# First batch of a random-feature attention and softplus block: the query features are turned before the division, and one product yields numerator and denominator

## The chip, the cores and the metric

One Trainium2 chip, one core. The metric is device time in microseconds (us) of the whole kernel, as the median of several executions. One execution is also profiled. In the profile PE is TensorE's matmul, PEld its weight load, DVE is VectorE, ACT is ScalarE, POOL is GpSimd and SP is the queue that issues transfers.

## The reference

```python
def phi(x):                                   # q and k, 8 batches x 8 heads x 576 tokens x 64
    proj = einsum('bhsd,md->bhsm', x, omega)  # 128 features
    h = proj - sum(x*x, -1)/2
    return exp(h - max(h, -1)) / sqrt(m)
q_p, k_p = phi(q_s), phi(k_s)
kv = einsum('bhsm,bhsd->bhmd', k_p, v)
z  = sum(k_p, axis=2)
num = einsum('bhsm,bhmd->bhsd', q_p, kv)
den = einsum('bhsm,bhm->bhs', q_p, z)[..., None] + 1e-06
x = transpose(num / den)                      # 4608 tokens x 512
h = x @ w_in                                  # 512 x 2048
out = (max(h, 0) + log1p(exp(-abs(h)))) @ w_out
```

All is float32. The two large products are made of three products each of rounded parts (a high and a low part of each operand).

## The kernel before

A "quad" is four heads of one batch, so there are 16 quads, two for each batch; the first batch is quads 0 and 1. A quad's 576 tokens are cut into five units `u` of 128 tokens (the last has 64 tokens, packed two heads deep, so it has half the instructions). The planner `in_order` takes a list of pieces of work (`do(engine, cost, due, emit, ...)`), each with an estimated cost, a due time, the pieces that it must follow (`after`) and the buffers that it takes and gives back, and writes one fixed order for all engines: at each step it picks an engine by the earliest start, and on that engine the startable piece with the earliest due time. A piece with two engines goes to the one that would end it first. `with_fill` puts idle matmuls (`fill`) into gaps of TensorE that it foresees, up to 228 us. The constants at the top (`AHEAD`, `LATE`, `PATIENCE`, `KEYS`, `QUERIES`, `IN`, `OUT`, `SPREAD`, `GAP`, `PACE`, and the offsets in `due + ...`) are these due times and margins.

In the first batch `plan_unit` loads a unit, projects it (`project`, lines 416 and 425), finds maxima and takes exponentials (line 454). Keys go on to `plan_early_keys`: `outer` (line 685) sums `kv` with its column of ones, `z` (line 700) and `high` (line 704) take it out of PSUM, `rows` (line 710) spreads z over all partitions by four matmuls, and `copy` (line 717) writes it as `zb`. Queries go to `plan_queries`: `den` (line 753) makes one multiply-and-sum of features and `zb` for each head on VectorE, `invert` (line 758) and `divide` (line 762) scale the features, `turn` (line 769) transposes them on TensorE, `turned` (line 781) copies them out, and `plan_x` multiplies them with `kvs` (line 871) for 256 or 320 tokens at once, which gives x with channels on the partitions, split into `xh` (line 883) and `xl` (line 887).

Later batches turn their features through memory instead, and stay on that way. The matmuls of the two large layers are lines 926 to 928 (`h`) and 955 to 957 (`acc`); the first two blocks of 256 tokens run side by side. The 32 weight pieces arrive in a packed form, and `plan_weights` unpacks and splits each on ACT, DVE and POOL (lines 306, 314, 317, 323, 326).

Of the kernel before, what the change touches and what calls it, by code (L numbers as in the profile page):

```python
# [10 lines left out]
F32 = mybir.dt.float32  # L11
# [34 lines left out]
PATIENCE = {"PE": 0.01, "DVE": 0.00, "ACT": 0.01, "POOL": 2.67, "SP": 0.97}  # L46
# [3 lines left out]
IN = (-36.40, -29.38, -35.24, 13.38, 39.26, -0.84, 18.43, 58.59, 71.95, 37.26, 72.53, 83.69, 168.77, 73.35, 60.09, 181.84)  # L50
OUT = (12.11, -3.45, -3.16, 37.83, 15.70, 36.06, 71.88, 74.85, 65.23, 26.71, 122.09, 40.54, 79.80, 155.65, 126.67, 119.25)
SPREAD = ((0, 24.76), (15.62, 68.69))
# [141 lines left out]
def favor_softplus_kernel(ctx, tc, q0, k0, qx, qy, kx, ky, vv, om, wi, wo, out):  # L194
# [37 lines left out]

    omf = const.tile([P, M], F32, name="omf")
# [54 lines left out]
    def plan_weights(nm, fc, due):  # L288
# [36 lines left out]
        def low_part(e):  # L325
# [5 lines left out]
            "SP", dma(0.65, 1.27, 1.7), due + 28.00, load, spare={} if last else {"w": 2},  # L331
# [5 lines left out]
        a = do(("ACT", "DVE"), (aw, dw2), due + 0.07, low_bits, after=[l], port=True)  # L337
        b = do("ACT", aw, due - 3.08, rebias, after=[l])
        c = do("DVE", dw, due + 2.51, joined, after=[a, b], port=True)
        d = do(  # L340
            ("ACT", "DVE"), (aw, dw2), due - 14.00, high_part, after=[c] + (in_w if last else []), take=[("w", box, "w")], port=True,
# [3 lines left out]
        return do(("DVE", "POOL"), (dw, pw), due - 10.48, low_part, after=[d], give=[(box, "raw")], port=True)  # L345


    class Quad:
        def __init__(self, n):
            self.b, self.qd = divmod(n, NQ)  # L350
            self.n, self.nm = n, f"_{self.b}_{self.qd}"
            self.kvm = self.zc = self.kvl = self.features = None
            self.keys, self.key_deps, self.part, self.sums = [], [], None, 0
            self.qt = ({}, {})
            self.turned, self.nums, self.slots = [], [], {}
            self.last = None
# [3 lines left out]
    def plan_unit(q, kind, us, due, early):  # L360
# [84 lines left out]
        def exponent(j):  # L445
# [12 lines left out]
            "SP", read(size), due + 9.90, load, behind=prev.get("load"),  # L458
# [3 lines left out]
        if kind == "k" and not early:  # L462
            for i in range(len(us)):
                ldv.append(do(
                    "SP", dma(0.7, 1.0, 0.7), due - 13.94, lambda i=i: load_v(i), behind=ld, take=[("v", b, ("vs", i))]
                ))
        s = do(("POOL", "ACT"), (pool(w), act(w)), due + 21.13, squares, after=[ld])
        r, sm = None, [("sm", b, "sms")]
        if not cols:
            r = do("DVE", dve(w), due + 115.69, norms, after=[s], behind=prev.get("norms"), take=sm)  # L470
# [3 lines left out]
            "PE", 0.19 + (0.46 if cols else 0.23) * nt, due - 6.73, project, after=[ld] + ([s] if cols else []),  # L474
# [5 lines left out]
        for j in range(2):  # L480
            e = do("DVE", dve(nt * M), due + 6.43, lambda j=j: maxima(j), after=[p] + ([r] if r and not j else []), behind=None if not j else e, give=[(b, "x")] if j and not early else [])
            es.append(e)
        e = do("DVE", 0.13, due - 29.30, less_norms, after=es, port=True)
        e = do("DVE", 0.13, due - 11.07, bias, after=[e], port=True)
# [9 lines left out]
        if kind == "k":  # L494
            plan_keys(q, us, due, b, es, ldv, early)
            return
        for i in range(len(us)):
            plan_queries(q, us[i], due - 7.44 * i, b, es, f"{nm}_{i}", i, i == len(us) - 1)

    def plan_split(q, kind, u, due):  # L500
# [59 lines left out]
        def exponent(t):  # L560
# [4 lines left out]
            "SP", read(n * (P + D) * P * 4), due - 77.07, load, behind=prev.get("load"), take=[("x", b, "x")],  # L565
        )
        prev["load"], ldv = ld, []
        if kind == "k":
            ldv = [do("SP", dma(0.7, 1.0, 0.7), due + 3.89, load_v, behind=ld, take=[("v", b, ("vs", 0))])]
        s = do(("POOL", "ACT"), (pool(n * D), act(n * D)), due + 7.71, squares, after=[ld])  # L570
        h = do(("ACT", "DVE"), (act(n * P), dve(n * P, 2)), due + 1.60, rounded, after=[ld], take=[("ts", b, "ts")], port=True)
        h = do(("DVE", "POOL"), (dve(n * P) + 0.12, 1.12 * pool(n * P)), due - 17.24, rest, after=[h, parted], give=[], port=True)
        r = do(
            "DVE", dve(n * D), due + 32.73, norms, after=[s, h], behind=prev.get("norms"), take=[("sm", b, "sms")],
# [10 lines left out]
        for t in range(n // 2):  # L585
            a = do(
                "ACT", act(2 * M, PSUM), due + 4.07, lambda t=t: aside(t), after=[p], behind=a,
                take=[] if t else [("ph", b, ("phs", 0))], spare={"ph": 1}, soon={} if t or n < 4 else {p: 0.22},
            )
            es.append(do("DVE", dve(2 * M), due - 13.77, lambda t=t: join(t), after=[a], give=[(b, ("ppb", t))]))  # L590
        m = do("DVE", dve(n * M), due + 26.68, maxima, after=es + [r])
        m = do("DVE", 0.33, due - 19.46, bias, after=[m], port=True)
# [20 lines left out]
    def plan_sums(q, keys, due, deps):  # L613
# [46 lines left out]
        for k, (b, i, u) in enumerate(keys):  # L660
            m = do(
                "PE", (0.86 if u < 4 else 0.43) + (0.0 if k else 0.09), due - 53.57, lambda k=k: outer(k), after=[m] if k else [x for x, _ in deps],
# [520 lines left out]
```

## Time and profile before

| | before |
|---|---|
| time, median of 3 | 1020.04 us (1019.51 to 1021.16) |
| profiled execution, time | 1019.18 us |
| profiled execution, span | 1017.4 us |
| mean granted TensorE clock | 0.994 of full |
| PE busy | 1005.5 us (99%) |
| PEld busy | 836.5 us (82%) |
| DVE busy | 764.1 us (75%) |
| ACT busy | 743.9 us (73%) |
| POOL busy | 106.2 us (10%) |

The span runs from the first to the last instruction; the time is 1.8 us longer. Busy shares are averages over the whole span: the first 80 us and the rest look different, and the rows below show both. In a line of the timeline the columns are start, length, engine, line and operation, and in brackets the idle time before it; the length of a matmul reaches past the start of the next, so that the pace is read from start to start. One float32 matmul that is no transpose stands as two records.

### The profile page before, as it was taken

The numbers are of one execution on the slowest core, as the hardware profiler recorded it, in microseconds if no ns is written. First come the engines' busy times: TensorE is split into PE (matmuls) and PEld (weight loads), VectorE is DVE, ScalarE is ACT, GpSimd is POOL, SyncE is SP. The second block draws the span as 40 slices with busy tenths as digits, with TensorE's granted clock in tenths as the row PEclk, the third lists the DMA queues.
The fourth block names the chain that finished last, engine by engine and source line by source line (L and its number), as shares of the span: only waits on it lengthen the run. The fifth ranks groups of instructions, "written<-read, shape, count | busy, mean of one in ns | idle before, by whom it ended". The sixth has DMA issues, their size and how long they took to land.

```text
span 1017.4 us, 17261 instructions
## 1 busy us (share of the span) xinstructions
PE 1005.5 (99%) x5424; PEld 836.5 (82%) x5424; DVE 764.1 (75%) x2320; ACT 743.9 (73%) x1857; POOL 106.2 (10%) x125
## 2 busy tenths in 40 slices
PE   8989999999999999999999999999999999999998
PEld 6768888888888888888788888888888878888886
DVE  5999977788979887889888878979798783223222
ACT  7999977777868776877778777877787765444443
POOL 1032113011001011001000110101001120000000
PEclk7999999999999999999999999999999999999999
DMA  9944245435354444445454354535263332001001
GB/s 339 374 151 151 71 144 144 135 105 144 109 169 132 123 133 148 130 112 137 120 157 122 112 141 128 164 105 159 73 189 106 96 101 83 1 1 42 1 1 41
DMA packets 117610, 124.48 MB, mean 122 GB/s; under 512 B 16272, under 2 KB 93712, under 8 KB 117520
## 3 DMA queue, kind: packets, MB, share of 16 engines
q1 hardware_dynamic: 117520, 123.39, 41.2%
q8 instruction: 43, 0.70, 0.3%
q14 instruction: 47, 0.39, 0.1%
HBM read 97.37 MB, written 25.98 MB: 121 GB/s over the span
## 4 chain that ended last, share of the span: by engine, by line
PE 95%; ACT 2%; DVE 1%; DMA 1%; SPq 0%; issue 0%; DVEq 0%
PE acc L955 13%; PE h L926 13%; PE acc L956 13%; PE acc L957 13%; PE h L927 13%; PE h L928 13%; PE kv_True L626 4%; PE xp L876 3%; PE ppq L538 3%; PE ppk L538 3%; PE kv_False L626 2%; PE ppq L416 1%; PE kv L685 1%; PE ppk L416 1%; DMA xq<-q 1%; DMA xk<-k 0%
## 5 line engine op out<-in xcount | busy, mean ns | idle before, releaser
L926 PE MATMUL h<-xh,wi 128*128 128x512 f32 (+1 forms) x640 | 238.4, 372 | 0.9 <-ACT qq L781 0.6
L927 PE MATMUL h<-xl,wi 128*128 128x512 f32 (+1 forms) x640 | 236.0, 369 | 0.0
L928 PE MATMUL h<-xh,wi 128*128 128x512 f32 (+1 forms) x640 | 235.8, 368 | 0.0
L955 PE MATMUL acc<-wo,gh 128*128 128x512 f32 x576 | 230.1, 400 | 0.0
L956 PE MATMUL acc<-wo,gh 128*128 128x512 f32 x576 | 225.5, 391 | 0.0
L957 PE MATMUL acc<-wo,gl 128*128 128x512 f32 x576 | 224.9, 390 | 0.0
L941 DVE SCALAR_TENSOR_TENSOR u<-h,u 128x512 f32<-128x512 f32 (+1 forms) x160 | 101.0, 632 | 113.0 <-ACT u L938 111.8
L932 ACT ACTIVATE u<-h 128x512 f32<-128x512 f32 (+1 forms) x160 | 89.2, 558 | 114.9 <-PE h L928 114.0
L945 ACT CAST gh<-u 128x512 fp32r<-128x512 f32 (+1 forms) x157 | 90.8, 579 | 65.7 <-DVE u L941 22.0
L926 PEld LDWEIGHTS h<-xh,wi 128*128 128x128 f32 x640 | 120.6, 188 | 22.1 <-DVE u L941 0.8
L928 PEld LDWEIGHTS h<-xh,wi 128*128 128x128 f32 x640 | 120.5, 188 | 20.6
L927 PEld LDWEIGHTS h<-xl,wi 128*128 128x128 f32 x640 | 120.7, 189 | 18.4
L955 PEld LDWEIGHTS acc<-wo,gh 128*128 128x128 f32 x576 | 108.3, 188 | 26.3 <-issue 7.1
L957 PEld LDWEIGHTS acc<-wo,gl 128*128 128x128 f32 x576 | 108.2, 188 | 24.0 <-DVE gl L949 0.4
L949 DVE TENSOR_TENSOR gl<-u,gh 128x512 fp32r<-128x512 f32 (+1 forms) x148 | 98.4, 665 | 37.6 <-ACT gh L945 33.2
L956 PEld LDWEIGHTS acc<-wo,gh 128*128 128x128 f32 x576 | 108.5, 188 | 18.0
L938 ACT ACTIVATE u<-u 128x512 f32<-128x512 f32 (+1 forms) x160 | 95.3, 596 | 2.3
L935 ACT ACTIVATE u<-u 128x512 f32<-128x512 f32 (+1 forms) x160 | 95.0, 594 | 2.7
L762 POOL TENSOR_TENSOR phq<-phq,dnq 128x512 f32<-128x512 f32 (+1 forms) x50 | 49.9, 1000 | 396.4 <-DVE dnq L758 290.7
L562 ACT ACTIVATE phk<-phk,smk 128x128 f32<-128x128 f32 x216 | 70.4, 392 | 12.1 <-DVE smk L558 11.8
L753 DVE CUSTOM_DVE_ANT_0 restq<-phq,zb 128x128 f32<-128x128 f32 x280 | 70.9, 290 | 8.4 <-ACT phq L562 4.8
L562 ACT ACTIVATE phq<-phq,smq 128x128 f32<-128x128 f32 x216 | 70.0, 392 | 4.0 <-DVE smq L558 3.9
(127 smaller groups left out, 1418.8 us busy)
## 6 DMA issues: line engine op xcount, KB each, us to landing
xk<-ky SPq DMA_DIRECT2D x48, 384.0 KB
xq<-qy SPq DMA_DIRECT2D x48, 384.0 KB
qdq<-restq SPq DMA_DIRECT2D x56, 256.0 KB
out<-o SPq DMA_DIRECT2D x36, 256.0 KB
vk<-vv SPq DMA_DIRECT2D x70, 130.0 KB
rawi<-wi SPq DMA_DIRECT2D x16, 512.0 KB
rawo<-wo SPq DMA_DIRECT2D x16, 512.0 KB
q<-qdq SPq DMA_DIRECT2D x64, 128.0 KB
```

What stands on the lines that cost most here:

```text
L562: nc.scalar.activation(b["ph"][:, c], b["ph"][:, c], AF.Exp, bias=b["sm"][:, 2, c : c + 1])
L926: nc.tensor.matmul(b["h"], wh, xh[:, cc, t], start=cc == 0, stop=False)
L927: nc.tensor.matmul(b["h"], wh, xl[:, cc, t], start=False, stop=False)
L928: nc.tensor.matmul(b["h"], wl, xh[:, cc, t], start=False, stop=cc == NCC - 1)
L935: nc.scalar.activation(b["u"], b["u"], AF.Exp, scale=-1.0)
L938: nc.scalar.activation(b["u"], b["u"], AF.Ln, bias=1.0)
L941: nc.vector.scalar_tensor_tensor(b["u"], b["h"], 0.0, b["u"], ALU.max, ALU.add)
L945: (nc.scalar.copy if e == "ACT" else nc.vector.tensor_copy)(b["gh"], b["u"])
L949: (nc.vector if e == "DVE" else nc.gpsimd).tensor_tensor(b["gl"], b["u"], b["gh"].bitcast(F32), ALU.subtract)
L955: nc.tensor.matmul(acc[tt], gh, w2[fc][:, 0], start=fc == 0, stop=False)
L956: nc.tensor.matmul(acc[tt], gh, w2[fc][:, 1], start=False, stop=False)
L957: nc.tensor.matmul(acc[tt], gl, w2[fc][:, 0], start=False, stop=fc == NFC - 1)
```

## The change

In the first batch the query features are no longer divided. `plan_early_queries` turns them on TensorE as they are, copies them out, and multiplies each head's turned features (now the stationary operand) with `kvs`, which holds the 64 columns of kv and z as a 65th: `num` gives numerator and denominator with tokens on the partitions. `invert` and `divide` then divide on VectorE, half as many elements as before. `plan_early_x` turns the quotient on TensorE (transposes of 128x128; for the last unit two matmuls with `stack`, two identities on top of each other) and splits it into `xh` and `xl`. So x of the first batch comes in three pieces of 256, 256 and 64 tokens for each quad, not in two of 256 and 320. `rows` and `copy` (the spread z) are gone. The last weight pieces' loads no longer wait for the product of quad 1. Nearly all due times and margins have other values.

```diff
-AHEAD = 375.50
+AHEAD = 374.44
-LATE = {"num": 1.22, "turn": 67.09, "project": 1.24, "blocks": 0.00, "out": 0.62, "in": 4.17, "store": 0.76, "outer": 0.20}
+LATE = {"num": 1.22, "turn": 66.91, "project": 1.24, "blocks": 0.00, "out": 0.81, "in": 4.17, "store": 1.97, "outer": 0.00}
-KEYS = ((-37.35, -23.60, -64.29, -37.35, -19.23), (-24.09, -26.58, -11.38, -11.52, -26.04))
-QUERIES = ((-156.79, -22.43, 15.03, 26.83, 24.93), (-27.14, -25.41, -47.26, 24.27, 28.98))
+KEYS = ((-34.89, -10.13, -62.32, -19.84, -30.15), (-27.37, -13.75, -11.38, -11.52, -45.48))
+QUERIES = ((-147.95, -33.19, 13.91, 26.44, 25.73), (-28.86, -31.76, -44.16, 21.32, 31.30))
-    GAP = 19.32
-    PACE = 4.69
+    GAP = 17.56
+    PACE = 4.80
...
+    stack = const.tile([P, D], F32, name="stack")
+    nc.vector.tensor_tensor(stack, eye[:, :D], eye[:, D:], ALU.add)
...
         def z():
-            q.z = z_wide[int(q.slots["z"][-1])][:, :4]
-            nc.vector.tensor_scalar(q.z, q.kv[:, :, 2 * D - 1], rm, None, ALU.mult)
+            x = at.tile([P, 4 * M], F32, name=f"kvs{q.nm}", tag=q.slots["zb"], bufs=1)
+            q.kvs = x[:, : 4 * (D + 1)].rearrange("p (c d) -> p c d", d=D + 1)
+            nc.vector.tensor_scalar(q.kvs[:, :, D], q.kv[:, :, 2 * D - 1], rm, None, ALU.mult)
-        def rows():
-            q.zp = bank(f"zp{q.nm}", q.slots["zp"])
-            for c in range(4):
-                nc.tensor.matmul(
-                    q.zp[:, c * M : (c + 1) * M], q.z[:, c : c + 1].broadcast_to([P, P]), ident,
-                    start=True, stop=True,
-                )
-        def copy():
-            q.zb = at.tile([P, 4, M], F32, name=f"zb{q.nm}", tag=q.slots["zb"], bufs=1)
-            nc.scalar.copy(q.zb.rearrange("p c m -> p (c m)"), q.zp)
...
+    def plan_early_queries(q, u, due, b, es, nm):
+        n = 4 if u < 4 else 2
+        def turn():
+            b["tp"] = bank(f"tp{nm}", b["tpb"]).rearrange("p (c m) -> p c m", m=M)
+            for c in range(n):
+                nc.tensor.transpose(b["tp"][:, c], b["ph"][:, c], ident)
+        def turned(e):
+            (nc.scalar.copy if e == "ACT" else nc.vector.tensor_copy)(b["junk"][:, :n], b["tp"][:, :n])
+        def num():
+            b["y"] = wide(bank(f"xn{nm}", b["yb"]))
+            for c in range(n):
+                o, h = (slice(c, c + 1), slice(c, c + 1)) if u < 4 else (slice(2 * c, 2 * c + 2), slice(c, 4, 2))
+                nc.tensor.matmul(b["y"][:, o], b["junk"][:, c], q.kvs[:, h], start=True, stop=True)
+        def invert():
+            dn = b["dn"] = at.tile([P, 4, 4], F32, name=f"dn{nm}", tag=b["dns"], bufs=1)
+            nc.vector.tensor_scalar(dn[:, 0], b["y"][:, :, D], 1e-6, None, ALU.add)
+            nc.vector.reciprocal(dn[:, 1], dn[:, 0])
...
+        def divide():
...
+            nc.vector.tensor_tensor(x, y, d, ALU.mult)
+        t = do("PE", 0.092 * n + 0.02, due + 9.98, turn, after=es, heat=256 * n, behind=prev.get("turn"), take=[("any", b, "tpb")])
+        h = do(("ACT", "DVE"), (act(n * M, PSUM), dve(n * M)), due - 43.63, turned, after=[t], give=[(b, "tpb")])
+        m = do(
+            "PE", 0.23 * n, due - 12.99, num, after=[h, q.kvl], heat=512 * n, take=[("any", b, "yb")],
+            behind=q.nums[-1] if q.nums else None, give=[(q.slots, "zb")] if u == NU - 1 else [],
+        )
+        i = do("DVE", 0.32 + (0.16 if u == 4 else 0), due - 58.05, invert, after=[m], take=[("dn", b, "dns")])
+        d = do("DVE", 0.09 + dve(4 * D), due - 54.18, divide, after=[i], give=[(b, "yb"), (b, "dns")])
...
+    def plan_early_x(q, due, o, rows, tail, nm):
+        w = D if tail else 2 * P
+        def turn():
+            y["x"] = bank(f"xp{nm}", y["b"])[:, : 2 * w].rearrange("p (a t) -> p a t", t=w)
+            for i, (b, _) in enumerate(rows):
+                for a in range(2):
+                    if tail:
+                        nc.tensor.matmul(y["x"][:, a], b["x_"][:, a], stack, start=True, stop=True)
+                    else:
+                        nc.tensor.transpose(y["x"][:, a, i * P : (i + 1) * P], b["x_"][:, a], ident)
+        def high(e):
+            (nc.scalar.copy if e == "ACT" else nc.vector.tensor_copy)(part(xh), y["x"])
+        def low():
+            nc.vector.tensor_tensor(part(xl), y["x"], part(xh).bitcast(F32), ALU.subtract)
...
-        if q.n == 1:
-            last_raw[1 if o else 0].behind = a
```

## Rows read from the trace of the kernel before

**Rows 1.** Windows: stretch, its length, busy us by engine (instructions), granted clock, DMA.

```profile
40.00:50.00 10.00, 9.64 (x73) 7.08 (x71) 9.27 (x48) 9.64 (x30) 2.14 (x2) 1.00 0.89 345
50.00:60.00 10.00, 8.21 (x63) 6.45 (x62) 9.68 (x43) 10.00 (x25) 3.77 (x3) 1.00 0.55 159
60.00:70.00 10.00, 8.65 (x63) 6.42 (x63) 9.90 (x42) 9.52 (x30) 3.40 (x4) 1.00 0.53 191
70.00:80.00 10.00, 9.43 (x78) 8.38 (x77) 9.87 (x23) 9.76 (x31) 0.92 (x1) 1.00 0.44 159
...
80.00:200.00 120.00, 120.00 (x827) 103.89 (x827) 98.16 (x303) 101.19 (x284) 23.68 (x26) 1.00 0.43 124
```

**Rows 2.** Windows of the fill matmuls alone (PE, PEld).

```profile
40.00:50.00 10.00, 1.40 (x4) 0.60 (x4) 1.00 0.89 345
50.00:60.00 10.00, 0.72 (x2) 0.30 (x2) 1.00 0.55 159
```

**Rows 3.** Windows of 2 us where the granted clock falls and comes back.

```profile
12.00:14.00 2.00, 0.04 (x1) 0.04 (x1) 1.94 (x6) 2.00 (x7) 0.00 (x0) 0.51 1.10 357
...
22.00:24.00 2.00, 2.00 (x19) 2.00 (x18) 1.93 (x4) 2.00 (x6) 0.00 (x0) 0.93 1.04 405
```

**Rows 4.** Timeline of PE, 0 to 90 us.

```profile
13.96 1.73 PE L416 MATMUL ppk<-omf,xk 64*128 64x128 f32 x8 [2.33 <-DMA xq<-q]
...
18.69 2.91 PE L1076 MATMUL fill<-ident 128*128 128x512 f32 x6
...
39.35 1.12 PE L685 MATMUL kv<-xk 128*128 128x128 f32 x8
40.30 0.60 PE L769 MATMUL tpq<-ident,xq 128*128 128x128 f32 x4
40.74 1.04 PE L685 MATMUL kv<-xk 128*128 128x256 f32 x4
...
43.85 1.08 PE L871 MATMUL xp<-qq,kvs 128*64 128x256 f32 x8
44.86 1.16 PE L710 MATMUL zp<-ident,z 128*128 128x128 f32 x8
45.77 0.70 PE L1076 MATMUL fill<-ident 128*128 128x512 f32 x2
...
51.41 0.63 PE L769 MATMUL tpq<-ident,xq 128*128 128x128 f32 x4 [1.41 <-DVE xq L762]
...
57.05 0.36 PE L926 MATMUL h<-xh,wi 128*128 128x256 f32 x1
...
75.22 0.39 PE L926 MATMUL h<-xh,wi 128*128 128x256 f32 x1 [0.57 <-ACT qq L781]
...
78.18 2.79 PE L626 MATMUL kv_True<-vk,phk 128*128 128x65 f32 x24
80.80 1.56 PE L626 MATMUL kv_False<-vk,phk 128*128 128x65 f32 x12
82.29 1.30 PE L871 MATMUL xp<-qq,kvs 128*64 128x320 f32 x8
```

**Rows 5.** Timeline of DVE: first of 16 sums in a run, and what follows.

```profile
46.96 0.29 DVE L753 CUSTOM_DVE_ANT_0 xq<-xq,zb 128x128 f32<-128x128 f32 x1
...
50.37 0.30 DVE L758 RECIPROCAL dnq<-dnq 128x4 f32<-128x4 f32 x3
...
55.92 0.75 DVE L887 TENSOR_TENSOR xl<-xp,xh 128x256 fp32r<-128x256 f32 x2
```

**Rows 6.** Groups by line, 0 to 80 us: count, busy us, mean ns, idle before.

```profile
L753 DVE CUSTOM_DVE_ANT_0 xq<-xq,zb 128x128 f32<-128x128 f32 (+1 forms) x40 | 10.5, 314 | 0.3 <-ACT xq L454 0.2
...
L762 POOL TENSOR_TENSOR xq<-xq,dnq 128x512 f32<-128x512 f32 (+1 forms) x5 | 5.3, 1077 | 31.9 <-DVE dnq L758 31.9
...
L762 DVE TENSOR_TENSOR xq<-xq,dnq 128x512 f32<-128x512 f32 x5 | 4.5, 893 | 0.0
```

**Rows 7.** The tile zb: count, duration ns min/median/max, first and last start.

```profile
L717 ACT COPY zb<-zp x2: 586/620/655, 36.2 to 46.3; 128x512 f32<-128x512 f32 x2
```

More of the change, by code (lines that the diff above doesn't have):

```diff
@@ L344, in plan_weights @@
             in_w.append(d)
[L345 removed]
+        return do(("DVE", "POOL"), (dw, pw), due - 13.42, low_part, after=[d], give=[(box, "raw")], port=True)
     class Quad:
@@ L457, in plan_unit @@
         ld = do(
-            "SP", read(size), due + 9.90, load, behind=prev.get("load"),
+            "SP", read(size), due + 9.68, load, behind=prev.get("load"),
             take=[("w" if early else "x", b, "x")], spare={"w": 2} if early else {},
@@ L564, in plan_split @@
         ld = do(
-            "SP", read(n * (P + D) * P * 4), due - 77.07, load, behind=prev.get("load"), take=[("x", b, "x")],
+            "SP", read(n * (P + D) * P * 4), due - 79.58, load, behind=prev.get("load"), take=[("x", b, "x")],
         )
@@ new lines, in plan_queries @@
+        d = do("DVE", 0.09, due + 4.11, invert, after=[d])
+        v = do(("POOL", "DVE"), (1.0 * f, dve(n * M)), due - 7.14, divide, after=[d], give=[(b, "dns")], port=True)
+        t = do("DVE", dve(n * M) + 0.03, due - 58.50, blocks, after=[v], port=True, late=LATE["blocks"], give=[(bu, ("phs", first))])
+        q.turned.append(
+            do("SP", dma(0.3, 0.95, 1.2, 1 if u < 4 else 2), due + 76.27, out_blocks, after=[t], give=[(bu, ("rest", first))], late=LATE["out"])
+        )
+        for o, w in chunks(q.b):
+            if (o + w - 1) // P != u:
+                continue
+            qc = {}
+            sizes = [w] if w <= 320 else [256, w - 256]
+            kinds = ["q" if w <= 256 else "q1"] if w <= 320 else ["q0", "q1"]
+            t = do(
+                "SP", dma(0.0, 0.0124 * w, 1.4, 4 * len(sizes)), due - 0.33, lambda qc=qc, o=o, sizes=sizes: in_blocks(qc, o, sizes),
+                after=list(q.turned), take=[(k, qc, ("tag", i)) for i, k in enumerate(kinds)], late=LATE["in"],
+            )
+            turned, q.turned = q.turned, [t]
+            plan_x(q, due, o, w, any_, qc, len(kinds))
+            q.turned = turned
@@ L841, in plan_queries @@
         t = do(
-            "PE", 0.092 * n, due + 5.12, turn, after=[v], heat=256 * n, behind=prev.get("turn"), give=[(bu, "x")] if last else [],
-            take=[(any_, b, "tpb")] + ([("q1" if u else "q0", qt, "tag")] if u in (0, 2) else []),
-            late=LATE["turn"] if q.b > 1 else 0,
-        )
-        prev["turn"] = t
-        h = do(
-            ("ACT", "DVE"), (act(n * M, PSUM), dve(n * M)), due - 46.49, turned, after=[t], give=[(b, "tpb")],
-        )
-        q.turned.append(h)
@@ L851, in plan_queries @@
-        if u not in (1, 4):
-            return
-        ch = 0 if u == 1 else 1
-        o, w = (0, 256) if ch == 0 else (256, 320)
-        plan_x(q, due, o, w, any_, qt)
-        q.turned = []
+            "PE", 0.23 if tail else 0.46, due - 36.01, turn, after=[d for _, d in rows], heat=1024, behind=prev.get("turn_x"),
+            take=[("any", y, "b")], give=[(b, "x") for b, _ in rows],
+        )
+        prev["turn_x"] = t
+        h = do(("DVE", "ACT"), (dve(2 * w), act(2 * w, PSUM)), due - 86.10, high, after=[t])
@@ L858, in plan_x @@
+        l = do("DVE", dve(2 * w), due - 89.86, low, after=[h], give=[(y, "b")])
+        for p in range(2):
+            x_lows[o, 2 * q.qd + p] = w, l
     def plan_x(q, due, o, w, any_, qt, nq=1):
```

182 lines of the change are left out of this document (79 added, 103 removed).

## The prediction

> **What bounds the kernel now.** I read the windows first, because busy shares over the whole span mix two stages. From 80 to 200 us PE is busy for all 120.00 us at full clock [rows 1]: there it is the limit, and work taken off another engine is worth nothing. Before that it is not. From 40 to 80 us PE is busy for 9.64, 8.21, 8.65 and 9.43 us of each 10, so it idles for 4.07 us, while DVE is busy for 38.7 of the 40 us and ACT for 38.9 [rows 1]. Of PE's busy time there, 1.40 and 0.72 us are fill matmuls, which compute nothing [rows 2]. So PE has 4.07 + 2.12 = 6.2 us without useful work between 40 and 80 us, set by DVE and ACT. The PE timeline names the places: it waits 1.41 us at 51.41 for a divide on DVE, and 0.57 us at 75.22, its last wait, for a copy on ACT [rows 4]. The first step of the large layer that has both quads' x stands at 57.05 [rows 4]. There is another soft stretch at the start: PE waits 2.33 us before 13.96 and runs 2.7 us of fill from 18.69 [rows 4], and the granted clock falls to 0.51 in 12 to 14 us and is back, at 0.93, in 22 to 24 us [rows 3]: half clock (1.2 GHz of 2.4) for about ten microseconds after an idle PE.
>
> So the account is PE's. After about 75 us it never waits, and the end moves by useful PE work added, less the empty PE time that disappears before.
>
> **The change part by part. PE, removed.** Four products with the divided features: one of 256 tokens takes 1.01 us from start to start (43.85 to 44.86); one of 320 tokens is 1.30 us long, less the same 0.07 us of overlap 1.23 [rows 4]. Two of each: 4.5 us. The spread of z takes 0.91 us (44.86 to 45.77) [rows 4], twice: 1.8 us. Together 6.3 us. The 36 transposes of features stay.
>
> **PE, added.** The product with numerator and denominator has 16 full and 2 x 2 half-unit matmuls a quad: 32 and 4 in all, each two records with 65 columns (130 in the last units) and 128 columns of weights. That shape is in the trace: 24 records of kv_True take 78.18 to 80.80, 0.109 us each; eight records of kv, entry included, take 0.95 us (39.35 to 40.30), 0.119 us each [rows 4]. I take 0.115: eight units of eight records at 0.92 us, 7.4 us. The two last units have four records of 130 columns: between 0.44 us (at 0.109) and the 1.04 us that four records of 256 columns last [rows 4]; by their closeness to 65 I take 0.5, 1.0 us together. So 8.4 us, with ends of 7.85 and 9.7. Turning the quotient: four transposes take 0.44 us (40.30 to 40.74) [rows 4], four times, and two last pieces of four records at 0.115: 1.8 + 0.9 = 2.7 us. Net 8.4 + 2.7 - 6.3 = **+4.8 us**, with ends of +4.2 and +6.1.
>
> The Trainium skill (TensorE: Matmul & The Clock Gate, Back-to-back issue gap) counts a warm matmul of up to 64 columns at about 60 cycles by its moving columns. By that, as an estimate from the page, the 72 records would take about 2 us, and PE's net would be about -1.6 us. The same page (LDWEIGHTS) lets the weight load go by the columns of the stationary operand, and the rows side with that: 0.109 us for 65 columns.
>
> **DVE, removed.** Forty sums: 16 of them take 46.96 to 50.37, 0.213 us each [rows 5], so 8.5 us; the group's busy time is 10.5 us, with some that lasted longer [rows 6]; I take 9.5. Ten reciprocals at 0.10 (three in 0.30) [rows 5]: 1.0. Five divides of 512 elements: 4.5 us [rows 6]. Together 15.0 us. **Added.** 22 small instructions, between 0.10 us each [rows 5] and twice that for reading PSUM: 2.2 to 4.4, taken as 3.0. Ten divides of 256 elements from PSUM, at 0.375 like the two of xl in 0.75 [rows 5]: 3.7. The split of x has the same elements in two instructions fewer. Net **-8.3 us** (-6.8 to -9.1). **ACT** loses two copies of zb, 0.62 us each [rows 7]: -1.2 us. **POOL** loses five divides, 5.3 us [rows 6]. So DVE and ACT together have 9.5 us less of the 77.6 us that they worked from 40 to 80 us. Both can do the unpacking of weights and the copies, so an even share is worth up to 4.8 us of that stage. PE cannot use all of it: it has 6.2 us empty and 4.8 us more to do.
>
> **Waits.** The features' transposes now follow the exponentials directly and wait neither for z nor for a sum. New is a visit: PE, ACT, PE (product), DVE, PE (quotient), then the split. PE is in order, so behind a product that waits for ACT's copy stand the projections and the steps of the large layer; a planner that expects the copy too early stops them all. Ahead of the full step at 57.05 go the 3.4 us of 16 sums and 0.9 us of spread z; the new products and divides of two units (2 x 0.92 us on PE, 2 x 0.7 us on DVE) come in, partly beside each other. I expect it about 2 to 4 us earlier. What is late next is weight unpacking on ACT and DVE, for which the 9.5 us are the cover; without them every one of the 4.8 us is paid.
>
> **Edits that I cost at nothing.** `stack` is one small DVE instruction before the first data; its cover is the wait for the first load. The last weight pieces' earlier loads fall among transfers that PE doesn't wait for in [rows 1] after 80 us; a late one there would show as PE idle time. The new due times keep the order of each chain; in the tail and after 80 us PE has no gap to lose. What they do before 31 us is open in sign: rival B.
>
> **Sum.** The empty time from 40 to 60 us (0.36 + 1.79 idle, 2.12 fill: 4.3 us) goes, as the waits on sums go; of the 1.92 us from 60 to 80 us I let half go, for DVE and ACT still run close to full there. Recovered 5.2. Then +4.8 - 5.2 = -0.4 us. The profiled execution took 1019.18 us (span 1017.4), 0.86 us less than the median shown, so 1019.18 - 0.4 + 0.86 = **1019.6 us**. About 0.2%, 2.04 us here, is what a measurement can tell from no change.
>
> **Rivals.** A is the forecast: trade of equal sizes, 1018.1 to 1021.7, chance 0.44.
>
> B, faster: the start gains too. With other due times, exponentials of keys come ahead of weight unpacking on ACT, so that PE doesn't stand still before 13.96 and keeps its clock. At most 2.33 us of wait and half of the 4.7 us from 13.96 to 18.69, together 4.7 us; at half of that, 2.4, the time is 1017.2. For it: ACT is full from 12 to 14 us while PE does nothing [rows 3]. Against: no new operation touches this stretch. Chance 0.35; it counts as faster from 1.7 us on.
>
> C, slower: the elementwise relief doesn't reach PE. ACT is as full as DVE [rows 1] and itself loses only 1.2 us; if the planner leaves unpacking on ACT, PE's gaps stay and the new matmuls are paid. With 0.7 us recovered, +4.1: 1024.1. It decides from where less than 2.8 of the 6.2 us are recovered. Against: DVE was the releaser of the longest wait [rows 4], and pieces go to whichever engine ends them first. Chance 0.13.
>
> D, slower: the clock falls again. In the trace it fell after 2.33 us without PE work and stayed low for some ten us [rows 3, 4]. If a wait for the new products does that between 45 and 60 us, where PE's useful work is 7.5 of 10 us, it costs about half of 7.5 us, 3.7: 1023.3. For it: fewer fills are there, and more hand-overs. Against: the clock stayed at 1.00 from 40 to 80 us through a wait of 1.41 us [rows 1, 4]. Chance 0.08. [...]
>
> **Numbers.** Faster 0.35 (B), within 0.2% 0.44 (A), slower 0.21 (C and D). The range 1016.0 to 1023.3 takes A, D's price and most of B, and leaves out B's far end and C, under 2 in 10.
>
> **What the profile after would show.** Right: records of the new product at 0.109 to 0.119 us; useful PE work up by 4 to 6 us; no CUSTOM sums before 90 us; DVE less busy by about 8 us in that stage; idle plus fill from 40 to 80 us near 1 us; last PE wait before 70 us. Wrong: idle plus fill above 3.4 us there (C); granted clock below 1.00 after 31 us (D); PE busy without a break from 12 to 20 us (B). A different PE pace after 80 us would overturn the account itself.

## The result, and the profile after

The changed kernel takes **1030.92 us** (median; 1020.19 for the kernel before beside it): a ratio of 1.0102, interval 1.0082 to 1.0122, so 1.0% slower where 1019.6 us was forecast. One of its four runs took 1908.22 us with a mean granted clock of 0.88 and is left out of the ratio, which rests on the three others (1030.23 to 1031.22). The profiled execution took 1030.23 us, its span is 1028.4 us, 11.0 more than before.

The windows of the changed kernel, with the columns of [rows 1]:

```profile
0.00:10.00 10.00, 5.52 (x21) 3.97 (x22) 4.21 (x17) 5.43 (x9) 2.02 (x8) 0.95 0.81 269
10.00:20.00 10.00, 10.00 (x47) 7.75 (x47) 3.74 (x13) 5.69 (x20) 2.24 (x4) 0.50 1.06 380
20.00:30.00 10.00, 10.00 (x55) 8.35 (x55) 4.81 (x20) 5.85 (x19) 0.61 (x1) 0.50 1.05 393
30.00:40.00 10.00, 10.00 (x55) 8.68 (x56) 6.39 (x23) 6.17 (x18) 2.88 (x4) 0.50 0.32 96
40.00:50.00 10.00, 10.00 (x77) 9.30 (x77) 6.93 (x22) 8.03 (x21) 0.32 (x1) 0.85 0.40 151
50.00:60.00 10.00, 10.00 (x86) 9.32 (x84) 8.39 (x23) 9.12 (x23) 1.27 (x1) 1.00 0.81 316
60.00:70.00 10.00, 9.55 (x86) 8.66 (x86) 9.26 (x33) 10.00 (x28) 1.28 (x1) 1.00 1.02 407
70.00:80.00 10.00, 10.00 (x86) 9.10 (x83) 9.18 (x24) 9.81 (x28) 3.84 (x3) 1.00 0.26 83
80.00:200.00 120.00, 119.73 (x850) 106.41 (x850) 99.84 (x317) 100.82 (x285) 27.01 (x32) 1.00 0.45 132
```

Against [rows 1], the middle stage did what was forecast: PE stands idle for 0.45 us between 40 and 80 us, and no fill runs there. But the granted clock is 0.50 (1.2 of 2.4 GHz) from 10 us to past 40 us, where before it was low for some ten [rows 3]. PE is 100% busy all that time, so a busy share alone shows nothing wrong. Its timeline does (start, length, what is run, idle time before it):

```profile
6.03 0.65 PE L427 MATMUL ppk<-halves,xk 128*128 128x56 f32 x4
9.66 2.93 PE L1103 MATMUL fill<-ident 128*128 128x512 f32 x6 [2.98 <-POOL ident L228]
12.52 1.23 PE L418 MATMUL ppk<-omf,xk 64*128 64x128 f32 x8
13.67 1.10 PE L427 MATMUL ppk<-halves,xk 128*128 128x56 f32 x4
...
37.05 1.23 PE L418 MATMUL ppq<-omf,xq 64*128 64x128 f32 x8
39.10 1.07 PE L815 MATMUL tpq<-ident,xq 128*128 128x128 f32 x4
39.97 3.44 PE L690 MATMUL kv<-xk 128*128 128x128 f32 x16
43.24 0.60 PE L815 MATMUL tpq<-ident,xq 128*128 128x128 f32 x4
...
63.83 0.36 PE L953 MATMUL h<-xh,wi 128*128 128x256 f32 x1
```

PE stands idle for 2.98 us until POOL has made the identity, which the planned fill matmuls read. From there every projection runs at half rate: 1.23 us for the eight records of a full unit and 1.10 us for its four sums, where the first unit of before takes 0.71 and 0.65:

```profile
5.27 0.71 PE L416 MATMUL ppk<-omf,xk 64*128 64x128 f32 x8
5.92 0.65 PE L425 MATMUL ppk<-halves,xk 128*128 128x56 f32 x4
```

Thirteen projections follow each other so, 12.52 to 39.10, with no key sum among them. The rate is back within the 16 key sums at 39.97. The full step of the large layer stands at 63.83 instead of 57.05 [rows 4].

Why the identity is late, on POOL (first two lines) and SP (the next three) of the changed kernel, and below them a line of POOL and one of SP of the kernel before:

```profile
8.29 0.61 POOL L402 TENSOR_TENSOR xk<-xk 128x256 f32<-128x256 f32 x1 [6.99 <-DMA xk<-k]
8.85 0.75 POOL L228 CAST ident<-eye 128x128 fp32r<-128x128 f32 x1
```
```profile
1.18 0.42 SPq L387 DMA_DIRECT2D xk<-k  x1
1.66 0.93 SPq L300 DMA_DIRECT2D rawi<-wi  x2
2.63 5.97 SPq L387 DMA_DIRECT2D xk<-k  x9
```
```profile
1.37 0.29 POOL L228 CAST ident<-eye 128x128 fp32r<-128x128 f32 x1
1.18 3.49 SPq L385 DMA_DIRECT2D xk<-k  x7
```

The due time of key unit 1 went from -23.60 to -10.13, so SP issues two weight pieces of 512 KB ahead of its load. POOL's square of that unit, now placed in front of the identity's cast, waits 6.99 us for it, and POOL works in order. Before, seven key units were loaded first and the cast stood at 1.37 us.

The ledger of PE by line over the first 200 us: projections and key sums 50.8 us before, 60.3 after (+9.5, the same records); new product and quotient 12.7 for 7.1 removed (+5.6); fills 8.8 to 6.7 (-2.1); idle 7.95 to 5.20 (-2.75). Together +10.3 of the 11.0 us: by so much less of the steady work fits into these 200 us. The half rate is the one large term; the other three nearly cancel (+0.8).

### The profile page after: what moved, and what is told of

Its sections match the earlier page's. It is cut to its first block, busy times and chain, and to the rows that moved or that the text cites. A ratio compares the mean times of both kernels' runs of the same rounds, so it can differ in the third digit from the quotient of the medians.

```text
span 1028.4 us, 17264 instructions
## 1 busy us (share of the span) xinstructions
PE 1018.0 (99%) x5466; PEld 851.5 (83%) x5466; DVE 756.1 (74%) x2254; ACT 738.5 (72%) x1846; POOL 109.8 (11%) x127
## 4 chain that ended last, share of the span: by engine, by line
PE 93%; ACT 2%; DVE 2%; DMA 1%; issue 0%; SPq 0%; POOL 0%; DVEq 0%; ACTq 0%
PE acc L982 13%; PE h L953 12%; PE acc L983 12%; PE h L954 12%; PE acc L984 12%; PE h L955 12%; PE kv_True L631 3%; PE xp L905 3%; PE ppq L543 2%; PE ppk L543 2%; PE kv_False L631 2%; PE ppk L418 1%; PE ppq L418 1%; PE kv L690 1%; PE ppk L427 1%; PE ppq L427 1%
## 5 line engine op out<-in xcount | busy, mean ns | idle before, releaser
L972 ACT CAST gh<-u 128x512 fp32r<-128x512 f32 (+1 forms) x152 | 88.5, 583 | 68.6 <-PE acc L984 24.5
L976 DVE TENSOR_TENSOR gl<-u,gh 128x512 fp32r<-128x512 f32 (+1 forms) x140 | 91.2, 652 | 32.8 <-ACT gh L972 31.7
L567 ACT ACTIVATE phk<-phk,smk 128x128 f32<-128x128 f32 x216 | 70.3, 393 | 12.8 <-DVE smk L563 12.7
```

Of the source, the lines that this page charges most:

```text
L567: nc.scalar.activation(b["ph"][:, c], b["ph"][:, c], AF.Exp, bias=b["sm"][:, 2, c : c + 1])
L976: (nc.vector if e == "DVE" else nc.gpsimd).tensor_tensor(b["gl"], b["u"], b["gh"].bitcast(F32), ALU.subtract)
```

## The experiments

Theory 1: the half rate at the start costs the time; it begins in the gap that the new due times open, and a stretch of projections alone keeps it. Theory 2: the new work or the new order costs the time, whatever the clock does. Each ratio is to the kernel before on the same chip (medians 1019.92 to 1020.63 us).

**Due times and operations apart.** Of the lines that both kernels have but for their numbers, 58, the numbers were exchanged, for example:

```
-            "PE", 0.87, due + 52.48, outer, after=es + [q.kvm], heat=2048,
+            "PE", 0.87, due + 46.42, outer, after=es + [q.kvm], heat=2048,
```

The new operations under the old due times:

> The changed operations under the old due times and margins wherever a piece of work exists in both kernels (58 places); only the new pieces keep their own. Cold-clock theory: the structure alone is worth what the account of TensorE says, 4.8 us added less some 5 recovered, 1018 to 1022 us. Theory that the new product costs the time: 1025 to 1031.

Measured: 1025.35 us (1024.19 to 1029.37), ratio 1.0060 [1.0037, 1.0082], inside the range of the theory that the new product costs the time. In its profile the new product and quotient take 13.0 us for 7.1 removed, but idle time in the first 200 us is still 7.6 us and fills 8.2: under the old due times almost nothing is recovered, and the added work is paid in full. The old operations under the new due times:

> The old operations under the new due times and margins (the same 58 places): the divided features, the sums on VectorE and the spread z are there again; three weight pieces are now loaded between the first and the second key unit. Cold-clock theory: the clock falls after the first key unit and the time is 1024 to 1031 us; as some key sums now stand between the projections, it may come back earlier than 43 us. Theory that the new product costs the time: 1019 to 1021.

Measured: 1032.09 us (1025.46 to 1038.85), ratio 1.0119 [1.0070, 1.0169]. Its windows:

```profile
10.00:20.00 10.00, 9.21 (x45) 7.44 (x45) 5.16 (x14) 7.06 (x23) 1.52 (x3) 0.56 1.07 374
...
60.00:70.00 10.00, 7.08 (x41) 5.71 (x41) 9.24 (x41) 9.48 (x25) 1.04 (x1) 0.79 0.31 110
```

Without one new operation the clock falls to 0.56 at the start, and the kernel loses as much as the changed one. Both mixtures are slower, though, and lose in the middle too (here 2.92 us of idle time in 60 to 70), since neither set of times was made for the other's operations: so this pair shows that the due times alone can cost 12 us, not how the 11 us divide.

**The gap alone.** The first planned fill group reads the zero tile instead of the identity, so PE needn't wait for POOL:

```
         fill("at.0", 8, idle)
+        early_fill = True
...
-                w[0](*w[1:])
+                w[0](*w[1:], idle if early_fill else dense)
+                early_fill = False
```

> The changed kernel, but the first planned group of six fill matmuls multiplies the zero tile that is ready at 1.4 us instead of the identity, so it need not wait for POOL. Cold-clock theory: PE's wait of 2.98 us after the first key unit is gone or under 1.5 us, the clock stays at 1.00 or is back before 25 us, and the time is 1020 to 1024 us. If the wait is not what cools the clock but the row of 14 projections is, the clock still stands at 0.5 for most of 12 to 40 us and the time is 1027 to 1030. Theory that the new product and its hand-overs cost the time: 1030 to 1031, whatever the clock does at the start.

Measured: 1022.78 us in the middle, in two groups: 1013.36 to 1015.49 (three runs, recorded clock 1.00) and 1020.87 to 1024.59 (seven, 0.99). The profile is of the first group (1015.49 us):

```profile
5.27 1.23 PE L418 MATMUL ppk<-omf,xk 64*128 64x128 f32 x8
7.30 2.91 PE L1103 MATMUL fill<-idle 128*128 128x512 f32 x6
...
11.19 0.65 PE L427 MATMUL ppk<-halves,xk 128*128 128x56 f32 x4
```

No gap, and full rate from about 11 us on. With every operation of the change in it, this group is 15 to 18 us faster than the changed kernel and 4 to 7 us faster than before: theory 2, by which the work costs the time whatever the clock does, fell. The slower group, of which there is no profile, is still 1 to 5 us above before.

**The old key times.** The changed kernel with the line `KEYS` of before:

> The changed kernel with the old due times of the ten key units (KEYS) and nothing else put back: seven key units are loaded ahead of the first weight pieces again, not one. Cold-clock theory: 1018 to 1022 us, the half clock lasts no longer than the ten us of before. Theory that the new product costs the time: 1029 to 1031.

Measured: 1022.77 us, ratio 1.0027 [1.0016, 1.0039], just above the cold-clock theory's range and far from the other's. And the same with 16 instead of 8 matmuls of the zero tile at the start:

> The changed kernel with the key units' due times of before (so that seven key units are loaded ahead of the first weights and the identity is made early) and 16 instead of 8 matmuls of the zero tile at the start. With the old key times alone the profile showed half rate from 5.3 to about 25 us and 1022.8 us. Theory 1 (the start's clock decides): with the longer start the full rate is there from about 7 us, and 1014 to 1018 us follow. Theory 2 (the old key times are worse for a reason of their own, as in transfers that come later): 1021 to 1024 us.

Measured: 1022.42 us, ratio 1.0024 [1.0013, 1.0034]. Theory 2's range came true, theory 1's did not. The longer start did give full rate from 7.22 us, but the old order of loads brings back the gap of the kernel before:

```profile
14.23 1.23 PE L418 MATMUL ppk<-omf,xk 64*128 64x128 f32 x8 [1.25 <-DMA xq<-q]
...
16.31 1.55 PE L418 MATMUL ppk<-omf,xk 64*128 64x128 f32 x8
```

From there the rate is half up to the key sums at 20.52. PE also idles for 2.8 us between 40 and 200 us, against 0.7 with the new key times. So the new key times seem to have a merit, apart from the late identity.

**What ends the half rate.** The first planned group of the changed kernel with 18 instead of 6 matmuls of the identity:

> The changed kernel with 18 instead of 6 matmuls in its first planned fill group (512 columns each, from the identity), nothing else. Theory 1 (what costs the time is the half rate that follows the 2.98 us gap, and projections alone do not end it): the late identity still leaves the gap, but the denser work lets the full rate (a projection of 8 in 0.72 us, not 1.23) be back before 20 us instead of 43 us; the fills cost 3 to 5 us, the 13 projections behind them win some 13 us: 1020 to 1026 us. Theory 2 (the time goes to the added product and to the new order, whatever the clock does): 12 more fills only cost, 1033 to 1036 us.

Measured: 1020.46 us (1019.41 to 1026.27), ratio 1.0014 [0.9999, 1.0028].

```profile
8.87 6.88 PE L1103 MATMUL fill<-ident 128*128 128x512 f32 x18 [1.34 <-POOL ident L228]
15.68 0.71 PE L418 MATMUL ppk<-omf,xk 64*128 64x128 f32 x8
...
25.91 1.22 PE L418 MATMUL ppq<-omf,xq 64*128 64x128 f32 x8
27.64 1.55 PE L418 MATMUL ppq<-omf,xq 64*128 64x128 f32 x8
29.12 1.10 PE L427 MATMUL ppq<-halves,xq 128*128 128x56 f32 x4
```

Twelve matmuls that compute nothing win 10 us: the rate is back behind them. But in this profile, of one of the two slowest of ten runs (1025.84), it falls again at 27.64, after ten projections. Only the start lengthened, 16 matmuls of the zero tile, the gap left in:

> The changed kernel with 16 instead of 8 matmuls of the zero tile at the start and nothing else: the first planned group still waits for the late identity. Theory 1 (gap, then projections): the longer start takes 2 to 4 us out of the 2.98 us gap, so the gap is 0 to 1.3 us; the rate is kept or soon back, 1015 to 1022 us. Theory 2 (the longer start only moves what follows): 1030 us or more, as in the changed kernel.

Measured: 1017.27 us (1014.70 to 1020.77), ratio 0.9970 [0.9956, 0.9984]. In its profile the gap is still 2.36 us, and after the planned group one projection is slow and the next is not: the half rate lasts 3.4 us, not 34. So the gap alone doesn't decide; what goes ahead of it counts too.

Both together, 16 at the start and the zero tile in the planned group:

> The changed kernel with 16 instead of 8 matmuls of the zero tile at the start, and the first planned fill group from that zero tile too, so that TensorE stands nowhere idle before 26 us. Theory 1: the two groups of times with the zero tile in the planned group (about 1014 and 1023 us) are a start at full rate from about 11 us and one at half rate to about 21 us; with twice the matmuls at the start the full rate is there in nearly every execution, the projections begin 2 to 4 us later, and the median is 1014 to 1018 us. Theory 2 (the two groups come from something later, such as the transfers): the two groups stay, moved by the 2 to 4 us, median 1022 to 1026 us.

Measured: 1018.50 us (1014.82 to 1020.09), ratio 0.9973 [0.9962, 0.9985], half a microsecond above theory 1's range; the next run repeated this program, since its edit named no unit that exists and added no instruction:

> The changed kernel with 16 matmuls of the zero tile at the start and the zero tile in the first planned group (1018.5 us median, 1014.8 to 1020.1), and besides one 512-column matmul of the zero tile ahead of each of the eight projections from key unit 1 of the second group of heads to the last query unit before the first key sum. In the profile of that kernel the rate fell at about 21.8 us with no idle time on TensorE, in the midst of the projections. Theory 1 (a stretch of nothing but projections does not hold the full rate, however busy TensorE is): the eight denser matmuls cost 1.7 to 2.2 us and hold it in every execution, so the times draw together at 1016 to 1018 us and none is above 1019. Theory 2 (the fall has another cause, such as what TensorE did before or the chip's other engines): the spread stays and moves up by 2 us, 1017 to 1022 us.

Measured: 1015.71 us (1015.51 to 1018.08), which says nothing of those eight matmuls. Over the 17 runs of this program: 1014.82 to 1020.09, median 1017.37. The profile of a slower one (1020.09) shows the fall:

```profile
20.67 1.22 PE L418 MATMUL ppq<-omf,xq 64*128 64x128 f32 x8
21.82 0.65 PE L427 MATMUL ppq<-halves,xq 128*128 128x56 f32 x4
22.41 1.30 PE L418 MATMUL ppq<-omf,xq 64*128 64x128 f32 x8
23.64 1.10 PE L427 MATMUL ppq<-halves,xq 128*128 128x56 f32 x4
```

It falls in the midst of projections, with no idle time right ahead of it. But one unit earlier, at 20.67, PE was held for half a microsecond: the unit takes 1.22 us at full rate (its sums take 0.65), because its third weight load starts 0.4 us after the second, with ACT as releaser. The run with 18 matmuls has the same hold at 25.91, a unit before its fall. Such a hold isn't enough by itself: the profiles of the zero-tile run (at 20.79) and of the longer start (at 23.70) have it too, and the rate stays.

**Denser work among the projections.** In `project`, ahead of the records of named units:

```
+            if nm in ("k_0_1_1", "k_0_1_2", "k_0_1_3", "k_0_1_4", "q_0_0_0", "q_0_0_1", "q_0_1_0", "q_0_1_1"):
+                nc.tensor.matmul(
+                    both[0].rearrange("p (a b) -> p a b", b=P), idle, idle.unsqueeze(1).broadcast_to([P, 4, P]), start=True, stop=True
+                )
```

> The changed kernel with 16 matmuls of the zero tile at the start, the zero tile in the first planned group, and now one 512-column matmul of the zero tile ahead of each of the eight projections from key unit 1 of the second group of heads on (the earlier edit of this kind named no unit that exists and added no instruction, so that its times were a repeat: 1014.8 to 1020.1 us over the 17 runs of that kernel). Theory 1 (a stretch of nothing but projections does not hold the full rate): the eight denser matmuls cost 1.7 to 2.2 us and hold it, so the times draw together at 1016 to 1018 us. Theory 2 (the fall has another cause): the spread stays and moves up, 1016 to 1022 us.

Measured: 1017.43 us (1015.70 to 1018.59), ratio 0.9976 [0.9967, 0.9985]. The rate held, but the spread stayed at three microseconds. The zero tile shares the place of the first V tile, and SP's load of it waited 3.8 us for the last of these matmuls, as the table of waits says. With the identity instead (`dense` for `idle`):

> As the run with the zero tile ahead of eight projections (1015.7 to 1018.6 us), but these eight matmuls read the identity instead. The zero tile shares its place with the first V tile, and in that run SyncE's load of V waited 3.8 us for the last of the eight matmuls, with 20 to 30 us at a DMA share of 0.74. Theory 1 (the rate is held, and what spread was left came from the late load): the wait is gone, the times draw together at 1015.5 to 1017.0 us, never above 1018. Theory 2 (the spread comes from elsewhere): 1015.7 to 1018.6 us as before, or more.

Measured: **1016.74 us (1015.67 to 1016.80)**, ratio 0.9966 [0.9952, 0.9979], none of its five runs beyond 1017. Its timeline at the same place:

```profile
22.66 0.48 PE L416 MATMUL ppq<-ident 128*128 128x512 f32 x1
23.07 0.72 PE L422 MATMUL ppq<-omf,xq 64*128 64x128 f32 x8
```

Of the fourteen projections up to the first key sum the full ones take 0.71 or 0.72 us and the two short ones 0.49. With one such matmul, 0.41 us from start to start, ahead of each of the last eight, the rate held through this profile. Whether it held because the work was denser isn't separated from another reading: the matmul added at 21.14 also stands where PE is held for half a microsecond without it (the unit behind it takes 0.72 us, not 1.22). The same into the changed kernel as it is, short start and gap left in, ahead of the eight key projections that follow the gap:

> The changed kernel as it is, with its short start and its late identity, and one 512-column matmul of the zero tile ahead of each of the eight key projections that follow the 2.98 us gap (units 2 to 4 of the first group of heads and all five of the second). Theory 1 (the half rate lasts for 30 us because the stretch holds nothing but projections): with a dense matmul ahead of each the rate is back within some of them, before 28 us instead of 43 us, and the time falls to 1020 to 1026 us for 2 to 4 us of added work. Theory 2 (after such a gap the rate stays low for a time that no work shortens): 1032 to 1034 us.

Measured: 1026.3 us in the middle, in two groups again: 1018.03 to 1020.49 (six runs) and 1032.11 to 1033.70 (six). The profiled run is of the first:

```profile
13.82 0.99 PE L431 MATMUL ppk<-halves,xk 128*128 128x56 f32 x4
14.63 0.48 PE L416 MATMUL ppk<-idle 128*128 128x512 f32 x1
15.04 0.71 PE L422 MATMUL ppk<-omf,xk 64*128 64x128 f32 x8
```

Its gap is 3.58 us, longer than in the changed kernel, yet the granted clock is back at about 14.5 us (0.93 in 14.5 to 15.0), before the first of the added matmuls starts at 14.63. So they did not end the half rate here. The other group, 2 us above the changed kernel, is theory 2's number: eight dense matmuls were paid and the time not won back. The run therefore doesn't show that denser work between projections ends the half rate once it lasts; the 12 more matmuls right behind the gap did. What decides between the two groups was not found. It also leaves open whether the changed kernel itself, of which three executions count, would show a faster group in more of them.

**The price of the new product, and the worth of the change.** In the program with 16 at the start and the zero tile, each matmul of the product issued twice, 36 more matmuls or 72 more records (`for c in list(range(n)) * 2:`):

> The kernel with the 16 matmuls of the zero tile at the start and the zero tile in the first planned group, and every product of the first batch (numerator and denominator in one) issued twice: 72 more matmuls, none used for another value. Its price against that kernel in the same call: +7.9 to +8.9 us if TensorE is the bound through the first batch (0.109 us a record and the reload of the weights, 8.9 us for 72 in the profile after the change), the step of the prediction that priced it at 8.4 us; 0 to +3 us if the engine had room there.

Measured: 1022.93 us (1022.37 to 1027.21), 4.4 us above the single product's median in the same call (1018.50), most of whose runs had lost their rate. Like with like: among runs with a recorded clock of 0.999 or more the median is 1022.54, that of the single product (both labels, two chips) 1015.53. That is 7.0 us for 72 records, 0.097 each, under the lower end expected (7.9) but far from the 0 to 3 us of an engine with room. PE is the bound there, as the account said.

The kernel before with 16 at the start, then once more (its added lines named no unit either, so the program is the same):

> The kernel before with 16 instead of 8 matmuls of the zero tile at the start, nothing else. Control: if the start alone held something for any kernel, before would gain too. Theory 1: before loses its rate at about 12 us, in the 2.33 us of waiting for the query load, and that gap shrinks by the 2 to 4 us that the longer start takes; the half rate of 12 to 22 us then goes in part, 1014 to 1020 us. Theory 2: nothing but the later start, 1020 to 1024 us.

> The kernel before with the same help as the changed one: 16 matmuls of the zero tile at the start and one ahead of each of the same eight projections. It tells what the change is worth where both keep their rate. Theory 1: before has a wait of 1 to 2 us for a query load or a square in the same stretch, so it keeps its rate in part and gains little: 1016 to 1020 us, and the changed kernel with the same help is 1 to 4 us faster. Theory 2 (the change is worth nothing or costs even with the clock kept): before with this help is at or below the changed one with it, 1013 to 1017 us.

Measured: 1019.37 us, ratio 0.9991 [0.9982, 0.9999], and 1019.78, 0.9994 [0.9985, 1.0003]. Its gap ahead of the second group of heads is still 1.22 and 1.57 us, and the rate still falls there. With the zero tile among its projections:

> The kernel before with 16 matmuls of the zero tile at the start and one ahead of each of the same eight projections. In before the rate falls in a wait of 1.2 to 1.6 us at 13 us, ahead of the first of these projections, and comes back at 21 to 24 us with the fills and key sums. Theory 1 (the change itself is worth some 4 us where the rate is kept): before is still at half rate for part of 14 to 24 us and pays for the eight matmuls where the rate is full, 1018 to 1022 us, above the changed kernel with the same help. Theory 2 (the change is worth nothing): at or below that kernel, 1014 to 1017 us.

Measured: 1029.37 us, ratio 1.0093 [1.0080, 1.0106], for a reason of its own. The waits of SP, 25 to 50 us, with total, count and longest:

```profile
SPq L393 <- PE ppq L414: 16.6, 1, 16.6
```

The load of V waited for the last reader of the zero tile, and all loads behind it on SP with it: in 30 to 40 us the DMA share is 0.01. It tells nothing of the change. Last, seven matmuls of the identity that cover the gap of before:

```
+            if nm in ("k_0_0_4",):
+                for _ in range(7):
+                    nc.tensor.matmul(
+                        both[0].rearrange("p (a b) -> p a b", b=P), dense, dense.unsqueeze(1).broadcast_to([P, 4, P]), start=True, stop=True
+                    )
```

> The kernel before with its rate kept: 16 matmuls of the zero tile at the start, and seven 512-column matmuls of the identity ahead of the last key projection of the first group of heads, so that they end about where the 1.2 to 1.6 us wait ends in which the rate falls (the run that put the zero tile ahead of eight projections of before held the V load for 16.6 us and told nothing). Theory 1 (the change itself is worth some 4 us when the rate is kept): before gains 0 to 3 us from its rate, 1016.5 to 1019.5 us, and stays above the changed kernel's 1015.5 us. Theory 2 (what the changed kernel wins is only the rate, the change is worth nothing): before comes down to 1014 to 1016 us.

Measured: 1019.22 us (1017.96 to 1019.42), ratio 0.9986 [0.9978, 0.9995]. The recorded clock is 1.00 up to 50 us, yet it wins only 1 us: its fills and added matmuls take 12.5 us for the 8.8 of before, and the middle stage still stands on DVE and ACT. Its window from 40 to 80 us, and below it that of the changed kernel with the identity among the projections:

```profile
40.00:80.00 40.00, 36.33 (x268) 28.72 (x265) 38.27 (x151) 38.64 (x111) 9.69 (x10) 0.96 0.63 224
```
```profile
40.00:80.00 40.00, 39.57 (x333) 36.18 (x332) 35.71 (x100) 38.86 (x104) 11.46 (x10) 1.00 0.71 263
```

PE idles for 3.67 us in the first, and its clock dips (0.83 in 50 to 60 us); in the second it idles for 0.43 us. With help for the rate on both sides the changed kernel is 2.5 us faster (1019.22 to 1016.74, on the same chip). As the worth of the change that is an estimate, for the help isn't the same on both sides and before still loses its rate once.

## Why the prediction was wrong

The step that failed is "Edits that I cost at nothing", in its last sentences: "The new due times keep the order of each chain; in the tail and after 80 us PE has no gap to lose. What they do before 31 us is open in sign: rival B." Left open in sign, only its gain was priced. The chain within one unit is kept, but not the order between POOL's square and the identity, between key loads and weights, or between projections and key sums; from these came a gap of 2.98 us and 34 us at half rate where before had ten, the +9.5 us of the ledger. The argument against rival B, that no new operation touches that stretch, was read as safety for the other sign too.

Point by point:

- **PE is the limit from 75 us on**: right. Idle time from 80 to 200 us is 0.27 us after the change, and doubling the product cost 7.0 us where the rate was held.
- **PE's net work**: about right. The new product was forecast at 8.4 us; its group in the changed kernel shows 8.9 us busy, the doubling 7.0. By line, 12.7 us came for 7.1 removed: +5.6 where +4.8 (+4.2 to +6.1) was said. (A quad has two half-unit matmuls, not the four of the prediction's wording; its sum counts them rightly.)

```profile
L824 PE MATMUL xnq<-kvs,xq 128*128 128x65 f32 (+1 forms) x72 | 8.9, 274 | 0.0
...
L869 PE MATMUL xpq<-ident,xq 128*128 128x128 f32 x16 | 2.6, 278 | 0.5 <-DVE xq L840 0.5
L867 PE MATMUL xpq<-stack,xq 128*128 128x64 f32 x8 | 1.2, 268 | 0.0
```

- The estimate by the Trainium skill (TensorE: Matmul & The Clock Gate, Back-to-back issue gap), 2 us for the 72 records, is about a quarter of what either measurement shows. The page gives that gap for a matmul by itself, without its weight load; here a weight load of 186 to 192 ns stands beside each record. The same page's LDWEIGHTS section has that load go by the columns of the stationary operand, 128 here, and the measured pace sides with it.
- **The empty time of the middle stage**: a little better than forecast. 5.2 of 6.2 us were to be recovered; 0.45 us is left between 40 and 80 us, though the stage starts later there. In the run with the identity among the projections the full step of the large layer stands at 50.05 us, 7.0 ahead of [rows 4], where 2 to 4 us were forecast; part of that is the faster start.
- **VectorE's relief**: right. Its busy time over the whole span went from 764.1 to 756.1 us, -8.0 where -8.3 was said; ACT's fell by 5.4, not 1.2.
- **Rival C** did not come in the changed kernel: idle and fill in that stage stayed far below its 3.4 us. It came with the new operations under the old due times: 4.3 us of idle and fill there, and 1025.35 us beside its 1024.1. So the relief reached PE by the new due times, not by the operations alone. **Rival D** had the right mechanism at the wrong place and size: the clock fell in a gap at the start, not between 45 and 60 us, and for some 34 us instead of ten.
- **Rival B** is what the changed kernel does once the rate is held: 1016.74 us beside the 1017.2 given to it. It is by the start, as B named, that the time is won. The windows of before, and below them those of the run with the zero tile in the first planned group (1015.49):

```profile
0.00:40.00 40.00, 36.12 (x256) 30.53 (x257) 28.46 (x105) 31.88 (x87) 4.17 (x13) 0.87 0.99 362
```
```profile
0.00:40.00 40.00, 38.45 (x289) 32.51 (x290) 30.48 (x105) 34.61 (x96) 8.30 (x17) 1.00 0.97 343
40.00:80.00 40.00, 39.55 (x333) 36.17 (x332) 35.99 (x99) 38.87 (x104) 12.49 (x11) 1.00 0.71 259
```

  Up to 40 us PE idles 2.3 us less, and the projections and key sums of the ledger take 49.2 us, 1.6 less, at the kept rate: 3.9 together, beside the 3.7 us by which this profile is faster than that of before (1019.18). From 40 to 80 us 3.6 us of idle time and 2.1 of fill go, 5.7 for 5.6 us of added work: the even trade of A.
- **The test named in the prediction**, "granted clock below 1.00 after 31 us (D)", is the one that caught it; [rows 3] had shown how much a wait of 2.33 us can cost.

Shown: the half rate at the start, with its gap, costs the time. The same operations with the rate held take 14 us less, and with the gap left in and the rate brought back behind it 10 us less. Not shown: whether it is the denser work or the covered holds that keep the rate among the projections. Argued only: that the order of loads, by the due time of key unit 1, is what makes the identity late. The run with the old `KEYS` has the early identity, but changes other key times with it; an identity made early with all else kept was not tried.

## What to carry to other kernels

Due times and priorities are edits like any other: before calling them free, walk each in-order engine and look for a small constant, such as an identity, that lands behind an instruction waiting for a load. A busy share of 100% doesn't say that TensorE runs at full rate; compare the length of one repeated group with its shortest in the trace. Where a kernel opens with small matmuls only, try a denser one between them, from a tile whose place no load is waiting for: here the times then lay within 1.1 us (five runs), without it within 5.3 (17 runs).

## What the runs showed of the hardware

- Half rate lasts under load. In the changed kernel TensorE was 100% busy with projections from 12.52 to 39.10 us at a clock of 0.50; it came back in key sums. The Trainium skill (TensorE: Matmul & The Clock Gate, HAM oscillation) tells of idle gaps as what throttles; here the rate also fell in the midst of projections, at 22.41 and 27.64 us in two of the profiles, where the only wait near was a hold of half a microsecond one unit before.
- The recorded clock isn't the whole truth. In the run with the old key times it reads 1.00 in 10 to 12 us, while the unit there takes the 1.23 and 1.10 us of half rate:

```profile
10.00:12.00 2.00, 2.00 (x14) 1.67 (x12) 0.93 (x6) 2.00 (x7) 0.00 (x0) 1.00 1.02 380
```
```profile
9.65 1.23 PE L418 MATMUL ppk<-omf,xk 64*128 64x128 f32 x8
10.81 1.10 PE L427 MATMUL ppk<-halves,xk 128*128 128x56 f32 x4
```

- The same program can fall into two groups of times, 1018 to 1020.5 and 1032 to 1034 us for the changed kernel with dense matmuls after its gap. Whether the eight matmuls at the start bring the full rate differs too: of the eight profiles with them, the changed kernel's among them, four have a first unit of 0.71 to 0.82 us and four one of 1.23 us. What decides it stays open.
